# Second and third stage of a Fourier filter: 64x32 and 32x64 tiles on TensorE, the complex sum on VectorE

## The chip, the cores and the metric

The kernel runs on one core of a Trainium2 chip. A core has TensorE (PE in the profiles; its weight loads are shown apart as PEld), VectorE (DVE), ScalarE (ACT), GpSimd (POOL) and SyncE (SP), which work side by side and wait for each other by semaphores, and a set of DMA queues. Matrix products go from SBUF into PSUM, which VectorE and ScalarE empty. The metric is the device time of one execution in microseconds: the median of several runs.

## What is computed

```python
def _attn_ref(x, filt_r, filt_i):          # x: 8 x 3008 x 256, filters: 1505 x 256
    X = np.fft.rfft(x, axis=1)
    F = (filt_r + 1j * filt_i)[None, :, :]
    Y = X * F
    y = np.fft.irfft(Y, n=x.shape[1], axis=1)
    return y.astype(np.float32)

def _moe_ref(x, w_in, w_out):              # x: 24064 x 256, w_in: 256 x 2048
    h = x @ w_in
    g = 0.5 * h * (1.0 + erf(h / sqrt(2)))
    return (g @ w_out).astype(np.float32)
```

Each of the 8 batches is filtered along its 3008 positions by a real Fourier transform, a product with one complex filter per frequency and channel, and the transform back. The result, 24064 rows in all, goes through a two-layer network with GELU.

## The kernel before

The transform of length 3008 = 47 x 64 is made of small matrix products. A batch passes four stages: `s1` (47-point sums, tiles of 47x64), `s2` (64-point sums that give the spectrum), the product with the filter, `s3` (64-point sums back) and `s4` (47-point sums back, which write the rows that the network reads). Between `s1` and `s2`, and between `s3` and `s4`, the data goes through DRAM (`R1`, `R2`) to change its layout. `fold` ahead of `s1` forms sums and differences of input rows on VectorE. Batch 0 has a path of its own (`c1` to `c4`), ahead of everything else; it shares buffers and the filter tile `F` with the others.

The network works in 47 tiles of 512 rows: `mm1` (L635) writes the hidden layer into PSUM banks of the kind `h` (three of them), ScalarE applies GELU (L638), and `mm2_seven` multiplies by `w_out` with seven products in place of eight, which needs sums of operands on VectorE (`sums_1` L676, `sums_2` L682, `sums_3` L689) and several combinations of its results (L722 to L736), which empty the two banks `ps_o`. There are three more banks, of the kind `f`, which the Fourier stages use, together with one `h` bank where they need four.

The order is written out by hand: the program is a list of slots, 16 for each tile of 512 rows (a slot takes some 0.83 us where nothing else is put in), and `put(slot, function, ...)` at the end of the kernel puts the Fourier work of batches 1 to 7 into slots between the network's. Every engine runs its instructions strictly in the order in which they were put.

What the change touches, per batch, in three rounds `u` = 0, 1, 2:

- `r1` (L441) reads `R1` into `b_sb`: four transfers of 384 KB, six frequencies each. Three are put in the same slot, the fourth one slot after the first round's `s2`, when a buffer has come free.
- `s2` (L448, matmuls at L458): 16 matmuls with 64 rows and 64 columns of weights (`T2p`) and 256 moving columns, in four tiles of the array. The 64 columns of weights are real and imaginary parts of one group of frequencies, so real and imaginary parts lie on different partitions of the four PSUM banks.
- `s2_out` (L462, VectorE at L470), four times a round, in slots 0, 2, 4 and 6 after `s2`: one bank, multiplied once by the real and once by the imaginary part of the filter (`F[:, 0]` and `F[:, 1]`, 1024 elements per partition in all), into the tile `p12`.
- `s3` (L473, matmuls at L484), 9 or 10 slots after `s2`: 16 matmuls with 64 rows and 64 columns of weights (`U`) and 512 moving columns. The 64 rows hold real and imaginary parts, and two matmuls that add into one bank (`t` = 0 and 1) take the two filter parts, so the sums of the complex product are made inside the matrix product.
- `s3_out` (L490) copies the four banks to SBUF on ScalarE (L329; one on VectorE) and writes them to `R2` from SP.
- `load_filters_again` (L129): after batch 0, `F` is filled anew in the layout that batches 1 to 7 need, from a copy in DRAM, by GpSimd's queue (slot 1) and SP's (slot 18).
- `load_next` (L151): a tiny copy on GpSimd (`gate`, L149) that waits for a product of `s2_out` holds back the loads of the next batch.

Of the kernel before, what the change touches and what calls it, by code (L numbers as in the profile page):

```python
# [10 lines left out]
ALU = mybir.AluOpType  # L11
FP32 = mybir.dt.float32
BF16 = mybir.dt.bfloat16
# [5 lines left out]
NA, NB = 47, 64  # L19
K1 = 24  # L20
# [11 lines left out]
class _Mix:  # L32
    def __init__(self, ctx, tc, x, filt_r, filt_i, w_in, w_out, out):
# [10 lines left out]
        self.pa = pool("pa", 3)  # L44
        self.pb = pool("pb", 3)
        self.pp = pool("pp", 3)
# [82 lines left out]
    def load_filters_again(self, eng, k0, k):  # L129

        for o in range(0, 128, 32):
            i = self.st["Fd"][o // 64, :, :, :, k0:k0 + k, :].rearrange("q i t k c -> (q i) t k c")
            f = self.F[o:o + 32, :, k0:k0 + k, :]
            if o < 64:
                eng.dma_start(out=f.rearrange("p t k c -> p t (k c)"), in_=i.rearrange("p t k c -> p t (k c)"))
            else:
                for t in range(2):
                    for e in range(2):
                        eng.dma_start(out=f[:, t, e::2], in_=i[:, t, 1 - e::2])

# [10 lines left out]
    def load_next(self, b, p, c, h):  # L151

        self.gate(self.st[b, "p", p][0:1, 0, 0:1])
        self.load_x_pairs(b + 1, c, h)
# [95 lines left out]
    def weights_4(self, g):  # L250


        ts = self.nc.gpsimd.tensor_scalar
        h, q, self.wt, self.wts = (g.tile([128, 1], FP32, name=n) for n in ("h48", "q48", "wt", "wts"))
        ts(out=h, in0=self.p, scalar1=48.0, scalar2=None, op0=ALU.is_ge)
        ts(out=q, in0=h, scalar1=-48.0, scalar2=-1.5, op0=ALU.mult, op1=ALU.add)
        self.nc.gpsimd.tensor_tensor(out=q, in0=self.p, in1=q, op=ALU.add)
        self.nc.gpsimd.tensor_tensor(out=q, in0=q, in1=q, op=ALU.mult)
        ts(out=q, in0=q, scalar1=2.25, scalar2=-1.0, op0=ALU.is_equal, op1=ALU.mult)
        ts(out=self.wt, in0=q, scalar1=2.0, scalar2=None, op0=ALU.add)  # L260
        ts(out=h, in0=h, scalar1=-2.0, scalar2=1.0, op0=ALU.mult, op1=ALU.add)
        self.nc.gpsimd.tensor_tensor(out=self.wts, in0=self.wt, in1=h, op=ALU.mult)
# [97 lines left out]
    def table_u_pick(self, g):  # L360
        to = self.cols
        self.nc.gpsimd.iota(to, pattern=[[0, 2], [64, 2], [33, 2], [2, 16]], base=0, channel_multiplier=0,
                            allow_small_or_imprecise_dtypes=True)
        self.pick = g.tile([128, 128], BF16, name="pick")
        self.nc.gpsimd.tensor_scalar(out=self.pick, in0=to, scalar1=self.p, scalar2=None, op0=ALU.is_equal)
# [7 lines left out]
    def table_4_rows(self, g):  # L373

        v = self.nc.gpsimd
        self.t4 = g.tile([96, 224], FP32, name="t4_sb")
        self.T1g = g.tile([NA, 2, 2, 12, 2, 2], BF16, name="T1g")
        self.T2g = g.tile([128, 2, 12, 2, 2], BF16, name="T2g")
        for x in range(2):
            for r in range(2):  # L380
                t = self.T1[0:NA, 24 * (x ^ r):24 * (x ^ r) + 24].rearrange("p (a k) -> p a k", k=2)
                for j in range(2):
                    v.tensor_copy(out=self.T1g[:, x, r, :, j], in_=t[:, :, ::-1] if j else t)
        t = self.T2.rearrange("p (a k) r j -> p r a j k", k=2)[:, 0, :, 0:2, :]
        for r in range(2):
            for j in range(2):
                v.tensor_copy(out=self.T2g[:, r, :, j], in_=t[:, :, j, ::-1] if j else t[:, :, j])

    def table_4_factors(self, g):
        ps = self.bank("ps_t4", "f")  # L390
        mm = lambda o, n, t, k: self.nc.tensor.matmul(ps[0:96, o:o + n], lhsT=t, rhs=self.eye[0:k, 0:k], start=True, stop=True)
        for x in range(2):
            mm(NA * x, NA, self.T1g[:, x].rearrange("p r a j k -> p (r a j k)"), NA)
        mm(128, 128, self.T2g.rearrange("p r a j k -> p (r a j k)"), 128)
        t = self.t4
# [44 lines left out]

    def r1(self, b, c):  # L441
        bt = self.pb.tile([128, 6, 256], BF16, tag="b", name="b_sb")
        self.st[b, "b", c] = bt
        v = self.st[b, "R1"].rearrange("n (r k) c -> (n r) k c", r=2)
        self.nc.sync.dma_start(out=bt, in_=v[:, 6 * c:6 * c + 6, :])


    def s2(self, b, u):  # L448

        nc = self.nc  # L450
        self.st[b, "ps2"] = ps = [[self.bank("ps_s2", "h" if i == d == 0 else "f") for d in range(2)] for i in range(2)]
        for i in range(2):
            for j in range(2):
                for odd in range(2):
                    for d in range(2):
                        k, r = 8 * u + 4 * i + 2 * j + odd, slice(64 * d, 64 * d + 64)
                        o = 64 * (odd ^ d)
                        nc.tensor.matmul(ps[i][d][o:o + 64, 256 * j:256 * j + 256],  # L458
                                         lhsT=self.T2p[r, k].rearrange("p a b c -> p (a b c)"),
                                         rhs=self.st[b, "b", k // 6][r, k % 6, :], start=True, stop=True)  # L460

    def s2_out(self, b, u, i, d):  # L462

        if d == 0:
            w = self.st[b, "w"] = self.pp.tile([128, 2, 4, 256], BF16, tag="p12", name="p12")
            for q in range(2):
                self.st[b, "p", 4 * u + 2 * i + q] = w[:, :, 2 * q:2 * q + 2].rearrange("p t a c -> p t (a c)")
        k = 8 * u + 4 * i + d
        ps = self.st[b, "ps2"][i][d].rearrange("p (a c) -> p a c", a=2)
        self.nc.vector.tensor_tensor(out=self.st[b, "w"][:, :, d:4:2, :], in0=ps.unsqueeze(1).to_broadcast([128, 2, 2, 256]),  # L470
                                     in1=self.F[:, :, k:k + 3:2, :], op=ALU.mult)

    def s3(self, b, u):  # L473

        nc = self.nc
        if u == 0:
            self.st[b, "R2"] = self.dram.tile([NB, 12, 4, 256], BF16, tag="R2", name="R2")
        ps = [[self.bank("ps_s3", "h" if i == par == 0 else "f") for par in range(2)] for i in range(2)]
        for i in range(2):
            for t in range(2):  # L480
                for q in range(2):
                    for par in range(2):
                        r = slice(64 * par, 64 * par + 64)
                        nc.tensor.matmul(ps[i][par][64 * q:64 * q + 64, :],  # L484
                                         lhsT=self.U[r, t].rearrange("p r w -> p (r w)"),
                                         rhs=self.st[b, "p", 4 * u + 2 * i + q][r, t, :], start=t == 0, stop=t == 1)
        self.st[b, "ps3"] = ps
        self.s3_out(b, u, 0)

    def s3_out(self, b, u, i):  # L490
        ps = self.st[b, "ps3"][i]
        vt = self.pv.tile([128, 4, 256], BF16, tag="v", name="v_sb")
        for par in range(2):
            self._evac(vt[:, 2 * par:2 * par + 2, :].rearrange("p a b -> p (a b)"), ps[par],
                       False if b == u == i == par == 1 else "act")
        for q in range(2):
            self.nc.sync.dma_start(out=self.st[b, "R2"][:, 4 * u + 2 * i + q], in_=vt[64 * q:64 * q + 64])

# [40 lines left out]
    def c1t(self, q, eng):  # L539

        b = self.st[0, "b", q] = self.pb.tile([128, 6, 256], BF16, tag="b", name="b_sb")
        ps = self.bank("ps_c1t", "n", BF16)
        for i in range(8):
            self.nc.tensor.transpose(ps[:, 128 * i:128 * i + 128],
                                     self.at[:, i % 2, 4 * q + i // 2].rearrange("c h n r -> c (h n r)"), self.eye)
        n = 1024 // len(eng)
        for i, e in enumerate(eng):
            self._evac(b[:, 0:4, :].rearrange("p a b -> p (a b)")[:, n * i:n * i + n], ps[:, n * i:n * i + n], e)

# [226 lines left out]
def kernel(  # L776
# [14 lines left out]
    g = m.small  # L791
# [112 lines left out]
    def put(slot, f, *a):  # L904
        at.setdefault(slot, []).append((f, a))
# [5 lines left out]
    for b in range(1, B):  # L911
# [5 lines left out]
        for c in range(4):  # L917
            slot = s1 + int(c * n1 + (b == 1 and c in (1, 2)))
            put((0, 1, 5, 8)[c] if b == 1 else (67, 69, 86, 94)[c] if b == 2 else s1 - 28 + e + 6 * c, m.fold, b, c)
            put(slot, m.s1, b, c)  # L920
            put(r1 if c < 3 else s2[0] + 1, m.r1, b, c)
        for u in range(3):
            put(s2[u], m.s2, b, u)
            for i in range(4):
                put(s2[u] + ((0, 2, 5, 6)[i] if b == u == 1 else 2 * i + (b == 2 and u == 0)), m.s2_out, b, u, i // 2, i % 2)
            s3 = s2[u] + (9 if b == 1 and u != 1 else 10)
# [40 lines left out]
    for i, slot in enumerate((15, 80, 96, 112)):  # L967
        put(slot, m.table_4_all, parts[2 * i:2 * i + 2])
    put(1, m.load_filters_again, nc.gpsimd, 0, 8)
    put(18, m.load_filters_again, nc.sync, 8, 16)  # L970
    put(20, m.weight_sums)
# [53 lines left out]
```

## Time and profile before

| | |
|---|---|
| runs | 744.07, 744.24, 745.28 us; median 744.24 |
| profiled execution | 743.4 us; its span from first to last instruction 741.6 us; mean granted clock 1.000 |
| second stage, L458 | 336 matmuls of 64x64x256, busy 13.4 us |
| third stage, L484 | 336 matmuls of 64x64x512, busy 22.2 us |
| products, L470 | 84 of 1024 elements, 1217 ns each, busy 102.0 us |
| bf16 sums of folding, L106 and L107 | 1024 elements, 680 to 717 ns each |
| network's first layer, L635 | busy 445.4 us; GELU, L638: 446.6 us, 602 ns each |
| F<-Fd, transfers | POOL: 2 of 256 KB and 8 of 64 KB; SP: 2 of 512 KB and 8 of 128 KB |
| b_sb<-R | 28 of 384 KB, 3.9 us to landing |

The page gives each engine's busy time and, as a chain, the work that ended last, followed back in time. The timeline lists instructions in order of their start, neighbours of one line merged. A number in brackets at the end of its lines is the idle time of the engine just before, with what ended it; a line without brackets followed the one ahead of it without a pause. An instruction's shown length reaches a little over the start of the next where the two don't depend on each other.

### The profile page before, as it was taken

The page shows a single profiled execution, that of the slowest core. Times are in us where ns is not written, and L with a number is a line of the kernel's source. Part 1 is how long each engine was busy: PE and PEld are TensorE (multiplying, and loading weights), DVE is VectorE, ACT ScalarE, POOL GpSimd, SP SyncE. Part 2 cuts the span into 40 slices and gives each one's busy share as a digit, 9 for nine tenths or more (in the row PEclk, how much of TensorE's full clock was granted, in tenths as well). Part 3 has the DMA queues.
Part 4 walks back from the last instruction along what each step waited for, and adds up shares of the span by engine and source line. Part 5 has one row for each costly group of instructions (what it writes and reads, how often), then busy time and mean ns, then how long its engine had stood idle before and what let it go on. Part 6 is the DMA issues. An engine that isn't in the chain of part 4 may idle for free.

```text
span 741.6 us, 20996 instructions
## 1 busy us (share of the span) xinstructions
PE 731.2 (99%) x8588; PEld 507.9 (68%) x8588; DVE 584.7 (79%) x1036; ACT 574.6 (77%) x1048; POOL 292.9 (39%) x546
## 2 busy tenths in 40 slices
PE   7999999999999999999999999999999999999997
PEld 4856665666776666666777666666677666777776
DVE  7986988889877897788976889678888887675666
ACT  6997778678877888777887778877888778777773
POOL 7995356674313452135511364115531212121121
PEclk9999999999999999999999999999999999999999
DMA  9999643646265643645626555255545443311011
GB/s 150 224 201 233 163 110 97 194 102 140 76 156 143 133 101 98 188 100 125 133 85 171 120 116 137 74 156 141 110 100 136 137 111 106 92 45 43 31 58 58
DMA packets 84051, 90.79 MB, mean 122 GB/s; under 512 B 13347, under 2 KB 63011, under 8 KB 83827
## 3 DMA queue, kind: packets, MB, share of 16 engines
q1 hardware_dynamic: 61011, 49.11, 25.8%
q0 software_dynamic: 22528, 40.15, 24.3%
q8 instruction: 67, 1.10, 0.6%
q14 instruction: 29, 0.24, 0.1%
q10 hardware_dynamic: 416, 0.20, 0.1%
HBM read 57.15 MB, written 48.23 MB: 142 GB/s over the span
## 4 chain that ended last, share of the span: by engine, by line
PE 93%; DVE 3%; ACT 2%; DMA 1%; POOL 0%; issue 0%; DVEq 0%; POOLq 0%
PE ps_h L635 42%; PE ps_o L707 39%; PE ps_s L484 3%; PE ps_s L513 3%; PE ps_s L429 2%; PE ps_s L458 2%; PE ps_o L648 1%; DMA x_sb<-in_x_dram 1%; PE ps_c L582 1%; ACT y_sb L329 1%; ACT g_sb L638 1%; DVE g_sb L682 1%; DVE s_sb L676 1%; PE ps_c L560 0%; PE ps_warm L323 0%
## 5 line engine op out<-in xcount | busy, mean ns | idle before, releaser
L638 ACT ACTIVATE g_sb<-ps_h 128x512 f16<-128x512 f32 x752 | 446.6, 602 | 146.3 <-PE ps_h L635 143.5
L635 PE MATMUL ps_h<-y_sb,w_in_sb 128*128 128x512 bf16 (+3 forms) x1600 | 445.4, 366 | 0.2 <-DVE a_sb L331 0.2
L754 POOL DMA_DIRECT2D out_dram<-ost x227 | 128.8, 574 | 389.4 <-DVE ost L736 368.6
L707 PEld LDWEIGHTS <-g_sb 128*128 128x128 f16 x2944 | 193.9, 98 | 83.6 <-issue 11.6
L707 PEld LDWEIGHTS <-s_sb 128*128 128x128 f16 x2208 | 148.0, 98 | 62.0 <-issue 11.1
L635 PEld LDWEIGHTS <-w_in_sb 128*128 128x128 bf16 x1600 | 125.1, 98 | 7.2 <-issue 1.1
L707 PE MATMUL ps_o<-w_sums,g_sb 128*128 128x128 f16 x1472 | 127.4, 219 | 1.1 <-DVE g_sb L682 0.9
L707 PE MATMUL ps_o<-w_sums,s_sb 128*128 128x128 f16 x1472 | 126.2, 219 | 0.0
L676 DVE TENSOR_TENSOR s_sb<-g_sb 128x1024 f16<-128x1024 f16 x184 | 120.5, 689 | 1.0 <-ACT g_sb L638 1.0
L707 PE MATMUL ps_o<-w_out_sb,g_sb 128*128 128x128 f16 x1472 | 118.9, 219 | 0.0
L470 DVE TENSOR_TENSOR p<-ps_s,F 128x1024 bf16<-128x1024 f32 x84 | 102.0, 1217 | 5.4 <-PE ps_s L458 4.0
L98 POOL DMA_DIRECT2D x_sb<-in_x_dram x156 | 79.0, 513 | 1.1 <-PE ps_c3t L597 0.8
L729 DVE TENSOR_TENSOR t_sb<-t_sb,ps_o 128x256 f32<-128x256 f32 x46 | 19.3, 420 | 60.2 <-PE ps_o L707 60.2
L682 DVE TENSOR_TENSOR g_sb<-s_sb,g_sb 128x1024 f16<-128x1024 f16 x92 | 65.0, 707 | 1.6
L689 DVE TENSOR_TENSOR s_sb<-g_sb 128x1024 f16<-128x1024 f16 x92 | 64.1, 696 | 0.0
L707 PE MATMUL ps_o<-w_out_sb,s_sb 128*128 128x128 f16 x736 | 63.8, 219 | 0.0
L736 DVE TENSOR_TENSOR ost<-t_sb,ps_o 128x256 f32<-128x256 f32 x90 | 33.7, 416 | 20.5 <-PE ps_o L707 20.5
L513 PEld LDWEIGHTS <-d_sb 96*128 96x128 bf16 x448 | 31.9, 98 | 25.3
L329 ACT ACTIVATE y_sb<-ps_s 128x376 bf16<-128x376 f32 x94 | 46.7, 497 | 3.2 <-PE ps_s L513 3.2
L329 ACT ACTIVATE v_sb<-ps_s 128x512 bf16<-128x512 f32 x83 | 45.0, 597 | 0.2
L331 DVE CAST a_sb<-ps_s 128x512 bf16<-128x512 f32 x54 | 34.7, 684 | 12.7 <-PE ps_s L429 12.4
L724 DVE TENSOR_TENSOR ost<-t_sb,ps_o 128x256 f32<-128x256 f32 x46 | 19.1, 415 | 26.1 <-PE ps_o L707 26.1
(155 smaller groups left out, 526.8 us busy)
## 6 DMA issues: line engine op xcount, KB each, us to landing
out_dram<-ost POOLq DMA_DIRECT2D x125, 128.0 KB, 2.3
b_sb<-R SPq DMA_DIRECT2D x28, 384.0 KB, 3.9
R<-v_sb SPq DMA_DIRECT2D x84, 128.0 KB, 2.4
d_sb<-R SPq DMA_DIRECT2D x56, 192.0 KB, 3.4
R<-a_sb SPq DMA_DIRECT2D x108, 96.0 KB, 2.2
x_sb<-in_x_dram POOLq DMA_DIRECT2D x48, 94.0 KB, 2.6
x_sb<-in_x_dram POOLq DMA_DIRECT2D x48, 48.0 KB, 2.7
x_sb<-in_x_dram POOLq DMA_DIRECT2D x12, 188.0 KB, 5.4
```

The costliest lines, as they stand in the source:

```text
L98: self.nc.gpsimd.dma_start(out=xt[64 * v + to:64 * v + to + m, h, 4 * c:4 * c + 4 * n, :], in_=xv[h][at:at + m, w:w + 4 * n, :])
L329: self.nc.scalar.activation(out=out, in_=in_, func=AF.Copy, scale=1.0 if scale is None else scale)
L331: self.nc.vector.tensor_copy(out=out, in_=in_)
L470: self.nc.vector.tensor_tensor(out=self.st[b, "w"][:, :, d:4:2, :], in0=ps.unsqueeze(1).to_broadcast([128, 2, 2, 256]), in1=self.F[:, :, k ...
L513: nc.tensor.matmul(ps[:, 94 * i:94 * i + 94], lhsT=d[:, (grp % 2) * 4 + i, 128 * half:128 * half + 128], rhs=self.T4a[:, 4 * grp + i], sta ...
L635: nc.tensor.matmul(ps[:, o:o + n], lhsT=w[:, dc], rhs=self.ring[:, dc, off:off + n], start=(dc == 0), stop=(dc == 1))
L638: nc.scalar.activation(out=self.st["g", t][:, jc, :], in_=ps, func=AF.Gelu)
L676: self.nc.vector.tensor_tensor(out=self.st["s", t][:, i:i + 2], in0=a, in1=b, op=ALU.subtract)
L682: self.nc.vector.tensor_tensor(out=a21[:, k], in0=self.st["s", t][:, k, 0], in1=a22[:, k], op=ALU.add)
L689: self.nc.vector.tensor_tensor(out=self.st["s4", t][:, k], in0=a12[:, k], in1=s2[:, k], op=ALU.subtract)
L707: nc.tensor.matmul(ps[:, (m + 1) % 2, sub, :], lhsT=a[:, i, 128 * sub:128 * sub + 128], rhs=b[:, i], start=i == 0, stop=i == 7)
L754: eng.dma_start(out=out, in_=tile_[lo - r0:lo - r0 + n])
```

## The change

For batches 1 to 7 the spectrum is laid out differently. In `s2` a matmul now takes 32 columns of weights, either those of the real (`x` = 0) or of the imaginary part (`x` = 1) of one parity of positions, and four groups of partitions hold four groups of frequencies, so that real and imaginary parts of a frequency lie side by side in one partition. There are 32 matmuls a round for 16, in tiles of 64x32. The filter product stays four instructions of 1024 elements a round; after every second one, two instructions are added that form the real part (a difference) and the imaginary part (a sum) of the complex product over 512 elements each, in place. `s3` then takes 32 rows (no more real and imaginary parts of the spectrum mixed in the rows) in tiles of 32x64: 16 matmuls of 512 columns as before, with the two passes `t` outermost. The lines of `R1` are read in six transfers of 256 KB (`pb` has four buffers of 4 x 256 in place of three of 6 x 256), and the filter tile holds each value once: a group of 32 partitions has 12 frequencies in place of 24. Tables (`table_u_pick`, `table_4_rows`, `table_4_factors`, `weights_4`) are put in the order that this needs, with as many instructions.

```diff
-        self.pb = pool("pb", 3)
+        self.pb = pool("pb", 4)
...
     def load_filters_again(self, eng, k0, k):
         for o in range(0, 128, 32):
-            i = self.st["Fd"][o // 64, :, :, :, k0:k0 + k, :].rearrange("q i t k c -> (q i) t k c")
-            f = self.F[o:o + 32, :, k0:k0 + k, :]
-            if o < 64:
-                eng.dma_start(out=f.rearrange("p t k c -> p t (k c)"), in_=i.rearrange("p t k c -> p t (k c)"))
-            else:
-                for t in range(2):
-                    for e in range(2):
-                        eng.dma_start(out=f[:, t, e::2], in_=i[:, t, 1 - e::2])
+            k1 = K1 // 2 * (o // 32 % 2) + k0
+            i = self.st["Fd"][o // 64, :, :, :, k1:k1 + k, :].rearrange("q i t k c -> (q i) t (k c)")
+            eng.dma_start(out=self.F[o:o + 32, :, k0:k0 + k, :].rearrange("p t k c -> p t (k c)"), in_=i)
...
     def load_next(self, b, p, c, h):
-        self.gate(self.st[b, "p", p][0:1, 0, 0:1])
+        self.gate(self.st[b, "p", p][0:1, 0:1])
...
-    def r1(self, b, c):
-        bt = self.pb.tile([128, 6, 256], BF16, tag="b", name="b_sb")
-        self.st[b, "b", c] = bt
-        v = self.st[b, "R1"].rearrange("n (r k) c -> (n r) k c", r=2)
-        self.nc.sync.dma_start(out=bt, in_=v[:, 6 * c:6 * c + 6, :])
+    def r1(self, b, u, e):
+        bt = self.pb.tile([128, 4, 256], BF16, tag="b", name="b_sb")
+        self.st[b, "b", u, e] = bt
+        v, k = self.st[b, "R1"].rearrange("n (r k) c -> (n r) k c", r=2), K1 // 2 * e + 4 * u
+        self.nc.sync.dma_start(out=bt, in_=v[:, k:k + 4, :])
...
     def s2(self, b, u):
-        for i in range(2):
-            for j in range(2):
+        for i in range(0, 4, 2):
+            for x in range(2):
                 for odd in range(2):
-                    for d in range(2):
-                        k, r = 8 * u + 4 * i + 2 * j + odd, slice(64 * d, 64 * d + 64)
-                        o = 64 * (odd ^ d)
-                        nc.tensor.matmul(ps[i][d][o:o + 64, 256 * j:256 * j + 256],
-                                         lhsT=self.T2p[r, k].rearrange("p a b c -> p (a b c)"),
-                                         rhs=self.st[b, "b", k // 6][r, k % 6, :], start=True, stop=True)
+                    for o in range(0, 128, 32):
+                        d, e = odd ^ (o // 64), o // 32 % 2
+                        r = slice(64 * d, 64 * d + 64)
+                        nc.tensor.matmul(ps[i + odd][o:o + 32, x],
+                                         lhsT=self.T2p[r, K1 // 2 * e + 4 * u + i + odd, x].rearrange("p q j -> p (q j)"),
+                                         rhs=self.st[b, "b", u, e][r, i + odd, :], start=True, stop=True)
...
-    def s2_out(self, b, u, i, d):
-        if d == 0:
-            w = self.st[b, "w"] = self.pp.tile([128, 2, 4, 256], BF16, tag="p12", name="p12")
...
-        self.nc.vector.tensor_tensor(out=self.st[b, "w"][:, :, d:4:2, :], in0=ps.unsqueeze(1).to_broadcast([128, 2, 2, 256]),
-                                     in1=self.F[:, :, k:k + 3:2, :], op=ALU.mult)
+    def s2_out(self, b, u, i):
+        if i % 2 == 0:
+            self.st[b, "w"] = self.pp.tile([128, 2, 2, 2, 256], BF16, tag="p12", name="p12")
+        w, v = self.st[b, "w"], self.nc.vector.tensor_tensor
+        k = 4 * u + i
+        self.st[b, "p", k] = w[:, 1, 1, i % 2]
+        v(out=w[:, :, :, i % 2], in0=self.st[b, "ps2"][i].unsqueeze(1).to_broadcast([128, 2, 2, 256]),
+          in1=self.F[:, :, k].unsqueeze(2).to_broadcast([128, 2, 2, 256]), op=ALU.mult)
+        if i % 2:
+            self.st[b, "y", k // 2] = w
+            for t, op in ((0, ALU.subtract), (1, ALU.add)):
+                o, z = (w[:, t, x].rearrange("p a c -> p (a c)") for t, x in ((t, 0), (1 - t, 1)))
+                v(out=o, in0=o, in1=z, op=op)
...
     def s3(self, b, u):
-        for i in range(2):
-            for t in range(2):
-                for q in range(2):
-                    for par in range(2):
-                        r = slice(64 * par, 64 * par + 64)
-                        nc.tensor.matmul(ps[i][par][64 * q:64 * q + 64, :],
-                                         lhsT=self.U[r, t].rearrange("p r w -> p (r w)"),
-                                         rhs=self.st[b, "p", 4 * u + 2 * i + q][r, t, :], start=t == 0, stop=t == 1)
+        for t in range(2):
+            for q in range(2):
+                for o in range(0, 128, 32):
+                    r = slice(o, o + 32)
+                    nc.tensor.matmul(ps[o // 32][64 * q:64 * q + 64, :], lhsT=self.U[r, t].rearrange("p r w -> p (r w)"),
+                                     rhs=self.st[b, "y", 2 * u + q][r, t, 0].rearrange("p a c -> p (a c)"),
+                                     start=t == 0, stop=t == 1)
...
-            put(r1 if c < 3 else s2[0] + 1, m.r1, b, c)
+        for u in range(3):
+            for e in range(2):
+                put(r1 if u < 2 else s2[0] + 1, m.r1, b, u, e)
...
-    put(1, m.load_filters_again, nc.gpsimd, 0, 8)
-    put(18, m.load_filters_again, nc.sync, 8, 16)
+    put(1, m.load_filters_again, nc.gpsimd, 0, 4)
+    put(18, m.load_filters_again, nc.sync, 4, 8)
```

The slots of `s2`, `s2_out`, `s3` and `s3_out` stay as they are.

## The prediction

> **What bounds the kernel now.** I read the page's first two parts, then the chain that ended last, then the timeline of VectorE (DVE) and TensorE (PE) around the stages that the diff touches.
>
> ```profile
> PE 731.2 (99%) x8588; PEld 507.9 (68%) x8588; DVE 584.7 (79%) x1036; ACT 574.6 (77%) x1048; POOL 292.9 (39%) x546
> ...
> PE 93%; DVE 3%; ACT 2%; DMA 1%; POOL 0%; issue 0%; DVEq 0%; POOLq 0%
> ```
>
> PE runs without a break and its stream is the time: what shortens it is gained whole, what makes it wait is lost whole. DVE's 79% is an average. In order of time the chain shows what one of the 21 rounds (7 batches, 3 rounds each) costs PE:
>
> ```profile
> 410.10 0.56 PE ps_s L458 x16
> 410.66 0.50 PE ps_o L707 x7
> ...
> 418.99 0.99 PE ps_s L484 x16
> 419.98 0.50 PE ps_o L707 x7
> ```
>
> Columns: start, length, what. The second stage (L458) takes 0.56 us, the third (L484) 0.99. Between them DVE has to turn the one's banks into the other's operand; its timeline in that round (start, length, idle time in brackets):
>
> ```profile
> 413.62 1.22 DVE L470 TENSOR_TENSOR p<-ps_s,F 128x1024 bf16<-128x1024 f32 x1
> 414.76 0.41 DVE L722 COPY t_sb<-ps_o 128x256 f32<-128x256 f32 x1
> 415.09 1.21 DVE L470 TENSOR_TENSOR p<-ps_s,F 128x1024 bf16<-128x1024 f32 x1
> 416.22 0.68 DVE L689 TENSOR_TENSOR s_sb<-g_sb 128x1024 f16<-128x1024 f16 x1
> 416.82 1.22 DVE L470 TENSOR_TENSOR p<-ps_s,F 128x1024 bf16<-128x1024 f32 x1
> 417.95 0.41 DVE L724 TENSOR_TENSOR ost<-t_sb,ps_o 128x256 f32<-128x256 f32 x1
> 418.40 0.42 DVE L727 TENSOR_TENSOR t_sb<-t_sb,ps_o 128x256 f32<-128x256 f32 x1
> ```
>
> No bracket: from the first product to the last, DVE has no idle time. The last product ends at 418.04, PE begins the third stage at 418.92. This **slack of 0.88 us** is all that may be added to DVE here. I took it from the same rows in every round: 0.88 or 0.89 in ten; 1.25 in four (batches 3 and 4, round 3; 5 and 6, round 2); batch 1: -0.05, -0.31, 0.80 (negative, since its last product is needed only halfway through the stage); batch 2 round 1: 0.39; batch 7: 1.16, 2.12, 2.19.
>
> **The change part by part.** *Third stage.* Still 16 matmuls of 512 columns, but eight tiles of 32x64 abreast for four of 64x64. Now four rows of four start 0.216 us apart (418.92, 419.17, 419.38, 419.60): 0.86 us, and 0.13 until the next form starts. Two rows of eight: 0.43 + 0.13. Neighbouring matmuls of four abreast start 3 ns apart, so four more cost 0.015: 0.575 us. Gain 0.415 x 21 = **-8.7 us**.
>
> *Second stage.* 32 matmuls of 256 columns for 16, again eight abreast: still four rows of 0.109 us, so 0.56 + 0.015: **+0.3 us**. Nothing in this trace runs more than four tiles abreast. The bounds: 0.575, if eight run as four do; 0.99, if only four run (eight rows of 0.109, and 0.13). I take 0.575, since weights and matmuls of four tiles already interleave at 3 ns without holding each other up.
>
> The Trainium skill speaks against that: TensorE Tiling, "Restrictions and Gotchas", says that different row tiles cannot access one PSUM bank at the same time. Before, each bank was written by one row group; now each of the second stage's banks is written from both, into different partitions. No row of this trace shows such a pair. By the rule the stage would run four abreast and the sum would be that of the third rival below; by the 3 ns rows it stays at 0.575.
>
> *Products.* Four per round, 1024 elements from PSUM, as before: 1.217 us each, unchanged.
>
> *Sums.* New: four per round, 512 bf16 elements. Nearest rows: the bf16 sums of folding (L106, L107: 1024 elements, 680 to 717 ns) and the f32 product of 512 (L569: 678 ns). By the first, 417 ns (half of 533 ns streaming, and 150 fixed); by the second, 678. I take 417: operands and output are like L106's. An operation that waits for nothing starts 0.08 us before the one ahead ends, so a sum occupies 0.336. The first of a pair reads the product just issued: like L727 behind L724 (ended 418.37, next 418.40) it starts 0.034 after that end, not 0.08 before. A pair delays what is behind it by 0.115 + 2 x 0.336 = **0.787 us**, and two pairs stand ahead of the third stage: its operand is ready 1.57 us later. Without the wait a pair would cost 0.67; by L569's price, 1.31.
>
> *What waits.* PE's third stage waits in order; behind it stand L707 and L635, so the whole of PE stops (and ACT, which lives on L635). The final sum is needed 0.22 us into the stage (its second row), and PE follows DVE by 0.05 (L682 ended 111.04, L707 went on at 111.09). So the wait is 1.57 + 0.05 - 0.22 - slack = 1.40 - slack: ten times 0.52, four times 0.16, then 1.46, 1.71, 0.60, 1.01, 0.24 and twice none: **+10.9 us**.
>
> *What is late next.* L722, L724 and L727 empty two ps_o banks. L722 is one pair late; it comes before the third stage, and a wait there only takes the place of part of that wait. L727 has over 2 us to spare in most rounds. Not in round 3 of batches 2 to 6, where folding of the next batch lies ahead of it:
>
> ```profile
> 448.87 0.68 DVE L106 TENSOR_TENSOR xs<-x_sb 111x1024 bf16<-111x1024 bf16 x1
> 449.59 0.69 DVE L107 TENSOR_TENSOR x_sb<-x_sb 111x1024 bf16<-111x1024 bf16 x1
> 450.20 0.41 DVE L724 TENSOR_TENSOR ost<-t_sb,ps_o 128x256 f32<-128x256 f32 x1
> 450.64 0.42 DVE L727 TENSOR_TENSOR t_sb<-t_sb,ps_o 128x256 f32<-128x256 f32 x1
> ```
> ```profile
> 451.66 0.33 PE L707 MATMUL ps_o<-w_sums,s_sb 128*128 128x128 f16 x3
> 451.83 0.39 PE L707 MATMUL ps_o<-w_sums,g_sb 128*128 128x128 f16 x4
> ```
>
> The matmul at 451.83 is the first into the bank that L727 leaves at 451.06: 0.77 us (1.13 in batches 3 and 4). DVE comes 1.57 later, PE only by what the round has cost so far (0.52 - 0.415 = 0.1; with 1.13 us: 0.16 - 0.415 = -0.25). It waits 1.62 - 0.77 - 0.1 = 0.75 us, and as much in the other two: 5 x 0.75 = **+3.7 us**.
>
> *What costs nothing.* Reading the spectrum: six transfers of 256 KB for four of 384 KB, two more SP issues of about 0.35 us; SP mostly waits, and the last two are still issued as soon as the second stage's first round frees buffers, two rounds ahead of need. Filters: half the bytes, and six issues fewer on POOL and on SP; PE waits for neither in the list of waits. Tables: as many copies of as many elements. POOL's gates come about 1 us later, and the loads behind them are for the next batch, 12 us or more ahead of its folding. ACT's first copy of the third stage starts as before, 0.65 us after the stage's start; PE then asks for the next banks 0.415 earlier, and GELU frees them 0.9 us ahead. If these covers fail I allow 1 us.
>
> *The sum.* -8.7 + 0.3 + 10.9 + 3.7 = +6.2 us. The profiled execution took 743.4 us (span 741.6, 1.8 around it): 749.6. It is 0.8 below the median of 744.24, on whose scale this is about **750 us**.
>
> **The rivals.** *1. DVE keeps up, and the third stage's gain stays: faster.* This is decided at the third stage of the ten common rounds: the sums cost no wait if a pair delays by no more than (0.88 + 0.22 - 0.05) / 2 = 0.52 us instead of 0.787, that is, if a sum takes 0.26 us or doesn't wait for its product. At 0.52 there remain 2.7 us of waits in batches 1 and 2 and 3 us at L727's bank: -8.4 + 5.7 = -2.7, on the median's scale 741.5; with nothing left to wait for, 735.8. For it: DVE has idle time after each round (1.70 us ahead of L729). Against it: that is after the third stage, not ahead of it.
>
> *2. Break-even.* Pairs at 0.67: a quarter of a microsecond less in each round that waits gives +1.5 to +2, 746.
>
> *3. Eight tiles don't run abreast in the second stage.* It takes 0.99, 21 x 0.43 = +9.0 us. DVE's start slips by half of that, which takes 0.22 off each wait; the sum becomes +11, 755. If the third stage fails too, +17 to +18, 762.
>
> **How the numbers follow.** My forecast (waits exceed the gain) 0.58, its own range 747 to 753, from pairs of 0.70 to 0.85. Rival 1: 0.20. Rival 2: 0.09. Rival 3: 0.13, most of it at 755. The range of 741.5 to 756 leaves out half of rival 1 and the extremes of 3 (and sums at L569's price, near 770). A measurement here can't tell 0.2% (1.5 us) from no change. Faster: 0.20, rival 1. Same: 0.09, rival 2's share. Slower: 0.71.
>
> **What would show it.** In the profile after: the third stage's 16 matmuls 0.57 us from end to end (0.99: rival 3); the second stage 0.57; sums of some 417 ns; the first of a pair 0.03 us behind its product's end; PE idle ahead of the third stage, released by the sums' line, some 0.5 us in common rounds and over 1 us in batch 1; PE idle at L707, released by L727's successor, in round 3 of batches 2 to 6. A DVE busy time near 615 us. I am wrong if PE shows no idle time released by the sums, or if a pair delays by 0.5 us or less.

## The result, and the profile after

The changed kernel takes 752.47 us (median of 4 runs, 752.39 to 753.63) against 744.15 (4 runs, 743.88 to 745.28): ratio 1.0112, interval 1.0095 to 1.0130. It is 8.3 us slower. The profiled execution took 752.45 us (span 750.5) against 743.4 (741.6): 9.05 us more, and this is the difference that the working below has to account for.

The page of the changed kernel, its busy times and the shares of the chain that ended last:

```profile
PE 726.4 (97%) x8782; PEld 508.1 (68%) x8924; DVE 616.0 (82%) x1120; ACT 574.8 (77%) x1048; POOL 287.3 (38%) x540
...
PE 75%; DVE 15%; ACT 3%; issue 2%; DMA 2%; POOL 2%; DVEq 0%
```

The trace holds 8782 matmuls for 8924 weight loads (8588 for 8588 before): 142 records are missing, 138 of them of the first layer, and the idle time that they leave is not idle time of the engine. So PE's busy time can't be set beside the 731.2 of before. The chain can: VectorE had 3% of it and has 15%, and the kernel without sums, further down, with as many records missing, has 4%. PE now waits for VectorE.

The groups of the changed lines, with shapes kept apart (busy us and mean ns of one; then the idle time before them). L464 is the product, L470 the sums, L453 the second stage, L482 the third:

```profile
L464 DVE TENSOR_TENSOR p<-ps_s,F 128x1024 bf16<-128x1024 f32 x84 | 102.2, 1219 | 3.1 <-PE ps_s L453 1.6
L470 DVE TENSOR_TENSOR p<-p 128x512 bf16<-128x512 bf16 x84 | 33.0, 434 | 1.4
L482 PE MATMUL ps_s<-p,U 32*64 32x512 bf16 x336 | 20.9, 392 | 0.7 <-DVE p L464 0.5
```

A sum takes 434 ns, and the 84 of them are busy for 33.0 us, about the 31.3 us by which DVE's busy time grew. The third stage's busy time fell by only 1.3 us (22.2 to 20.9), because the shown lengths of the matmuls that have started the stage, some 390 ns each, reach over the wait of the later ones for their operand. What one round costs is seen in PE's timeline, in the round that the prediction used (start, length):

```profile
426.81 0.59 PE L633 MATMUL ps_h<-y_sb,w_in_sb 128*128 128x512 bf16 x2
427.34 1.02 PE L482 MATMUL ps_s<-p,U 32*64 32x512 bf16 x16
428.29 0.56 PE L705 MATMUL ps_o<-w_sums,s_sb 128*128 128x128 f16 x7
```

From the stage's start to the next matmul it is 428.29 - 427.34 = 0.95 us; it was 0.99. Where nothing waits (batch 7, rounds 2 and 3) the same distance is 0.57. So here 0.385 us of the stage is waiting, inside the group, and no bracket shows it. VectorE in the same round:

```profile
421.89 1.22 DVE L464 TENSOR_TENSOR p<-ps_s,F 128x1024 bf16<-128x1024 f32 x1
423.14 0.76 DVE L470 TENSOR_TENSOR p<-p 128x512 bf16<-128x512 bf16 x2
423.82 0.42 DVE L720 COPY t_sb<-ps_o 128x256 f32<-128x256 f32 x1
424.15 1.22 DVE L464 TENSOR_TENSOR p<-ps_s,F 128x1024 bf16<-128x1024 f32 x1
425.28 0.68 DVE L687 TENSOR_TENSOR s_sb<-g_sb 128x1024 f16<-128x1024 f16 x1
425.88 1.22 DVE L464 TENSOR_TENSOR p<-ps_s,F 128x1024 bf16<-128x1024 f32 x1
427.14 0.76 DVE L470 TENSOR_TENSOR p<-p 128x512 bf16<-128x512 bf16 x2
427.81 0.41 DVE L722 TENSOR_TENSOR ost<-t_sb,ps_o 128x256 f32<-128x256 f32 x1
428.26 0.42 DVE L725 TENSOR_TENSOR t_sb<-t_sb,ps_o 128x256 f32<-128x256 f32 x1
```

From a product to the evacuation behind its pair of sums it is 423.82 - 421.89 = 1.93 us, where it was 1.14: a pair delays by 0.79. The last pair ends at 427.90, half a microsecond after PE has begun the stage that reads it.

The waits that the prediction did not have are brackets in PE's timeline, in batch 1 round 3, batch 2 round 1 and batch 7 round 1:

```profile
100.80 0.45 PE L705 MATMUL ps_o<-w_out_sb,g_sb 128*128 128x128 f16 x5 [0.64 <-DVE ost L734]
...
154.32 0.34 PE L511 MATMUL ps_s<-T4a,d_sb 96*128 96x94 bf16 x4 [1.68 <-DVE p L464]
...
603.78 0.44 PE L705 MATMUL ps_o<-w_out_sb,g_sb 128*128 128x128 f16 x5 [0.64 <-DVE ost L734]
```

The first and the last are a bank that L734 empties, with a pair of sums ahead of it on DVE. The middle one is the fourth stage, which wants a bank of kind `f` that a late product still holds. There VectorE itself was slow:

```profile
148.74 1.22 DVE L464 TENSOR_TENSOR p<-ps_s,F 128x1024 bf16<-128x1024 f32 x1
149.99 1.83 DVE L470 TENSOR_TENSOR p<-p 128x512 bf16<-128x512 bf16 x2
151.74 1.30 DVE L687 TENSOR_TENSOR s_sb<-g_sb 128x1024 f16<-128x1024 f16 x1
152.97 1.21 DVE L464 TENSOR_TENSOR p<-ps_s,F 128x1024 bf16<-128x1024 f32 x1
```

A pair takes 1.83 us for 0.76, and L687 1.30 for 0.68, while GpSimd builds the fourth stage's table beside them:

```profile
148.78 1.62 POOL L405 TENSOR_TENSOR tmp_sb<-t_sb 96x376 f32<-96x376 f32 x2
150.48 1.05 POOL L407 TENSOR_TENSOR T4a<-tmp_sb 96x376 bf16<-96x376 f32 x1
151.62 2.12 POOL L405 TENSOR_TENSOR tmp_sb<-t_sb 96x376 f32<-96x376 f32 x2
```

### The profile page after: what moved, and what is told of

It reads as the page before. It is cut to its first block, busy times and chain, and to the rows that moved or that the text cites. A ratio compares the mean times of both kernels' runs of the same rounds, so it can differ in the third digit from the quotient of the medians.

```text
span 750.5 us, 21598 instructions
## 1 busy us (share of the span) xinstructions
PE 726.4 (97%) x8782; PEld 508.1 (68%) x8924; DVE 616.0 (82%) x1120; ACT 574.8 (77%) x1048; POOL 287.3 (38%) x540
## 3 DMA queue, kind: packets, MB, share of 16 engines
q8 instruction: 70, 1.15, 0.6%
## 4 chain that ended last, share of the span: by engine, by line
PE 75%; DVE 15%; ACT 3%; issue 2%; DMA 2%; POOL 2%; DVEq 0%
PE ps_o L705 33%; PE ps_h L633 31%; DVE p L464 5%; PE ps_s L511 3%; PE ps_s L424 2%; ACT g_sb L636 2%; PE ps_s L482 2%; DVE s_sb L674 2%; DVE p L470 1%; POOL out_dram L752 1%; DMA x_sb<-in_x_dram 1%; ACT v_sb L324 1%; PE ps_s L453 1%; PE ps_o L646 1%; DVE g_sb L680 1%
## 5 line engine op out<-in xcount | busy, mean ns | idle before, releaser
L633 PE MATMUL ps_h<-y_sb,w_in_sb 128*128 128x512 bf16 (+3 forms) x1462 | 415.8, 365 | 0.6 <-DVE a_sb L326 0.2
L674 DVE TENSOR_TENSOR s_sb<-g_sb 128x1024 f16<-128x1024 f16 x184 | 119.7, 685 | 0.9 <-ACT g_sb L636 0.9
L464 DVE TENSOR_TENSOR p<-ps_s,F 128x1024 bf16<-128x1024 f32 x84 | 102.2, 1219 | 3.1 <-PE ps_s L453 1.6
L687 DVE TENSOR_TENSOR s_sb<-g_sb 128x1024 f16<-128x1024 f16 x92 | 63.9, 694 | 0.0
L727 DVE TENSOR_TENSOR t_sb<-t_sb,ps_o 128x256 f32<-128x256 f32 x46 | 19.3, 420 | 41.9 <-PE ps_o L705 41.9
L734 DVE TENSOR_TENSOR ost<-t_sb,ps_o 128x256 f32<-128x256 f32 x90 | 33.7, 417 | 18.4 <-PE ps_o L705 18.4
L511 PE MATMUL ps_s<-T4a,d_sb 96*128 96x94 bf16 x448 | 38.1, 206 | 2.6 <-DVE p L464 1.7
```

The costliest lines, as they stand in the source:

```text
L464: v(out=w[:, :, :, i % 2], in0=self.st[b, "ps2"][i].unsqueeze(1).to_broadcast([128, 2, 2, 256]), in1=self.F[:, :, k].unsqueeze(2).to_broad ...
L511: nc.tensor.matmul(ps[:, 94 * i:94 * i + 94], lhsT=d[:, (grp % 2) * 4 + i, 128 * half:128 * half + 128], rhs=self.T4a[:, 4 * grp + i], sta ...
L633: nc.tensor.matmul(ps[:, o:o + n], lhsT=w[:, dc], rhs=self.ring[:, dc, off:off + n], start=(dc == 0), stop=(dc == 1))
L674: self.nc.vector.tensor_tensor(out=self.st["s", t][:, i:i + 2], in0=a, in1=b, op=ALU.subtract)
L687: self.nc.vector.tensor_tensor(out=self.st["s4", t][:, k], in0=a12[:, k], in1=s2[:, k], op=ALU.subtract)
```

## The experiments

Eight kernels ran, the first four on one chip (the kernel before there: 743.84 us) and the last four on another (744.03); ratios are to these, and plain differences between kernels of different series carry the 0.3 us by which the kernel before differs among them. The loss of a round, below, is by how much PE falls behind the kernel before from this round's second stage to the next round's; it is read from the starts of the network's second-layer matmuls, which are the same in both profiled executions. The theory: VectorE's sums, 0.79 us a pair, make TensorE wait, and take back more than the new third stage gives.

**No sums.** In `s2_out` of the changed kernel the loop goes.

```diff
-            for t, op in ((0, ALU.subtract), (1, ALU.add)):
-                o, z = (w[:, t, x].rearrange("p a c -> p (a c)") for t, x in ((t, 0), (1 - t, 1)))
-                v(out=o, in0=o, in1=z, op=op)
```

> The changed kernel without the difference and the sum on VectorE (84 instructions less): the output lacks the cross terms of the complex product. Theory (all of the loss is PE waiting for what VectorE does late because of the sums; the tile forms themselves are a gain): nothing of the waits is left, third stage 0.57 us in all 21 rounds, 744.2 - 8.7 + 0.3 = 735.8 us (735 to 737.5). Rival (the new tile forms, the new reads of R1 or the new filter loads cost something themselves): 740 us or more.

735.94 us, ratio 0.9897 (0.9882 to 0.9912). Each group of third-stage matmuls, shapes kept apart:

```profile
L479 PE MATMUL ps_s<-p,U 32*64 32x512 bf16 x336 | 13.8, 386 | 0.0
```

The stage is busy 13.8 us for 22.2 before and 20.9 with the sums. It takes 0.570 in every round but batch 1's first two, and from batch 2 round 1 on each round brings PE 0.42 us forward of the kernel before. So the new tiles alone, with the new reads and filter loads, are worth 7.9 us, and the sums cost 8.3 + 7.9 = 16.2.

**The sums twice.** Each line is issued a second time.

```diff
                 v(out=o, in0=o, in1=z, op=op)
+                v(out=o, in0=o, in1=z, op=op)
```

> Each sum is issued twice (the second adds or subtracts once more, so the output has the cross terms twice). Theory (VectorE's time ahead of the third stage sets the wait): a pair delays by another 0.67 us, a round by 1.34 us, and every one of the 19 rounds that wait now loses all of it: 752.5 + 19 x 1.34 = 778 us, a little more where VectorE no longer catches up between rounds (776 to 786). Rival (the wait comes from the semaphores and the order, not from VectorE's time): 752 to 760 us.

796.5 us (794.0 to 798.0), ratio 1.0718 (1.0700 to 1.0736): slower as foretold, by more than foretold. VectorE's timeline, a doubled pair in a round of batch 5:

```profile
448.55 0.42 DVE L470 TENSOR_TENSOR p<-p 128x512 bf16<-128x512 bf16 x1
449.01 0.42 DVE L471 TENSOR_TENSOR p<-p 128x512 bf16<-128x512 bf16 x1
449.35 0.42 DVE L470 TENSOR_TENSOR p<-p 128x512 bf16<-128x512 bf16 x1
449.80 0.42 DVE L471 TENSOR_TENSOR p<-p 128x512 bf16<-128x512 bf16 x1
450.14 0.41 DVE L721 COPY t_sb<-ps_o 128x256 f32<-128x256 f32 x1
```

A repeated sum reads what the one before it wrote, so it starts 0.46 us after it and not 0.34. From the first sum to the evacuation it is 1.59 us, where it was 0.68: a doubled pair delays by 0.91 us more, and the expectation counted 0.67. Two pairs in 21 rounds are 2 x 0.91 x 21 = 38 us, which gives 791, and common rounds lose just that, 1.94 us for 0.11. Two rounds lose more: batch 2 round 1, 6.5 us for 1.89 (2.8 beyond the doubled pairs), and batch 1 round 3, 4.0 for 1.0 (1.2 beyond). Most of this is not VectorE's: TensorE's granted clock, 1.00 throughout in the changed kernel, is 0.50 here from 104.8 to 108.2 us and from 166.2 to 169.6, just behind the third stages of these two rounds, which take 2.96 and 5.08 us. In the first stretch PE falls back by 1.2 us, in the second by 1.5; another 0.9 in batch 2 round 1 is a wait of the second stage for `b_sb`, and some 0.4 is left for sums that GpSimd stretches. Why the clock fell there and not behind other long stages (3.86 us in batch 1 round 1) is open. In common rounds each further microsecond on VectorE ahead of the third stage is lost once TensorE waits.

**The same sums in the kernel before.** After every second product of the old kernel, a difference and a sum of the same size, in place.

```diff
+        if d:
+            w = self.st[b, "w"]
+            for t, op in ((0, ALU.subtract), (1, ALU.add)):
+                o, z = w[:, t, 0:2].rearrange("p a c -> p (a c)"), w[:, 1 - t, 2:4].rearrange("p a c -> p (a c)")
+                self.nc.vector.tensor_tensor(out=o, in0=o, in1=z, op=op)
```

> The kernel before, with a difference and a sum of 512 bf16 elements in place after every second product, at the same places in VectorE's order as in the changed kernel (the output then has terms mixed that don't belong together). Theory, by the same steps as the prediction: the old third stage needs the late operand only 0.45 us (difference) and 0.66 us (sum) after its start, so in common rounds it doesn't wait; what is left are the banks that VectorE empties late: 0.14 us in ten common rounds, 0.5 to 0.85 in round 3 of batches 2 to 6, 1 to 2 in batch 1 and in batch 2 round 1, 0.6 in batch 7 round 1: together some +10 us, 754.5 us (752 to 757). Rival (the shorter third stage is a full gain of 8.4 us that simply adds to the cost of the sums): 752.5 + 8.4 = 761 us.

754.69 us (754.17 to 755.29), ratio 1.0149 (1.0134 to 1.0164), as the theory has it; the rival that adds the parts up (761) falls. PE's timeline in batch 5 round 1:

```profile
427.79 1.09 PE L489 MATMUL ps_s<-p,U 64*64 64x512 bf16 x16
428.81 0.56 PE L712 MATMUL ps_o<-w_sums,s_sb 128*128 128x128 f16 x7
```

With the sums ahead of it the old third stage takes 1.02 us and the new one 0.95. The old stage is slow to reach its late operand anyway: it waits 0.03 where the new one waits 0.385. The faster stage is worth 7.9 us alone, and only 754.7 - 752.5 = 2.2 beside the sums; for the rest it has the wait in its place.

**The third stage later.** Its slot goes two back in batches 2 to 6, behind the wait.

```diff
-            s3 = s2[u] + (9 if b == 1 and u != 1 else 10)
+            s3 = s2[u] + (9 if b == 1 and u != 1 else 12 if 1 < b < B - 1 else 10)
```

> The changed kernel with the third stage two slots later (12 in place of 10 after the second stage) in batches 2 to 6. Theory: the wait of some 0.38 us ahead of the third stage goes in the rounds 1 and 2 that have it, the waits at the banks of ps_o stay, above all in round 3 of each batch, where L725 lies behind the folding: 752.5 - 3.1 = 749.4 us (748.3 to 750.5). Rival (the wait only moves to what comes next, for VectorE lacks time over the whole round): 752 us or more.

754.54 us (753.72 to 754.68), ratio 1.0145 (1.0129 to 1.0160): the theory's number is wrong, and the rival, that the wait only moves, is right. PE's timeline in batch 5 round 1:

```profile
428.63 0.33 PE L705 MATMUL ps_o<-w_sums,s_sb 128*128 128x128 f16 x3
429.12 0.40 PE L705 MATMUL ps_o<-w_sums,g_sb 128*128 128x128 f16 x4 [0.16 <-DVE t_sb L725]
429.35 0.59 PE L633 MATMUL ps_h<-y_sb,w_in_sb 128*128 128x512 bf16 x2
429.88 0.64 PE L482 MATMUL ps_s<-p,U 32*64 32x512 bf16 x16
430.45 0.56 PE L705 MATMUL ps_o<-w_sums,g_sb 128*128 128x128 f16 x7
```

The third stage is at its 0.57 in all 15 rounds that were moved. But a matmul ahead of it waits for the bank that L725 empties: from the three matmuls to the four behind them it is 0.49 us, 0.17 in the changed kernel (the bracket shows only part of the wait). Common rounds lose 0.06 us in place of 0.11, and round 3 of each of the five batches 0.5 more than in the changed kernel: 5 x 0.5 - 10 x 0.05 = 2.0, as far as the medians lie apart (2.1). The two profiled executions differ by 1.3: this one also loses 0.4 us less ahead of the first changed round, and 0.5 less in batch 2 round 1, where a wait for `b_sb` has come in the place of others. The list of waits of this kernel, and then of the changed one (waiting line, what it waited for: us in total, times, longest):

```profile
PE ps_o L705 <- DVE t_sb L725: 8.2, 12, 1.5
```
```profile
PE ps_o L705 <- DVE t_sb L725: 3.1, 5, 0.6
```

In the kernel before, L727 (here L725) left its bank 2 us ahead of need, and I took that for room. The third stage's own 0.99 us lay between the two and was part of it: take the stage out from there and the room goes with it. What is late is VectorE, by two pairs, and whoever asks for its results first pays.

**Half of each sum.** 256 of the 512 elements.

```diff
-                v(out=o, in0=o, in1=z, op=op)
+                v(out=o[:, 0:256], in0=o[:, 0:256], in1=z[:, 0:256], op=op)
```

> Each sum over 256 of its 512 elements (half of the cross terms are left out). A pair then delays by about 0.115 + 2 x 0.20 = 0.52 us, the point that the prediction named as the one from which the common rounds no longer wait at the third stage. Theory: third stage 0.57 to 0.60 us in the ten common rounds; waits stay in batch 1, in batch 2 round 1 and, of 0.3 us, in round 3 of batches 2, 5 and 6; sum -0.8 us against the kernel before: 743.4 us (742 to 745). Rival (each added instruction costs PE by itself, whatever its length): 750 us or more.

740.7 us (740.18 to 741.13), ratio 0.9953 (0.9938 to 0.9967): below the expectation of 742 to 745. VectorE and PE in batch 5 round 1:

```profile
417.71 0.48 DVE L470 TENSOR_TENSOR p<-p 128x256 bf16<-128x256 bf16 x2
418.11 0.41 DVE L722 TENSOR_TENSOR ost<-t_sb,ps_o 128x256 f32<-128x256 f32 x1
```
```profile
418.27 0.64 PE L482 MATMUL ps_s<-p,U 32*64 32x512 bf16 x16
```

A pair delays by 0.51 us (0.11 and 0.40 from its start to L722's) in place of 0.79, and the third stage runs at 0.57 in all rounds of batches 3 to 7. So with a pair of 0.51 us the common rounds don't wait, and with one of 0.79 they wait 0.52: this fits the 0.52 us a pair that the prediction's first rival named, though nothing between 0.51 and 0.79 was run. The rival's own number for that case, 741.5, was 0.8 too high. The expectation of this run was further off and its sum isn't itemized, so where it failed is open. By rounds the ten common ones gain 0.42 us each, batch 1 loses 0.27, 0.53 and 0.22, and batch 2 round 1 loses 0.62, with 1.0 us of waiting for `b_sb` in it.

**GpSimd's table later.** The last of four pieces of table work goes from slot 112 to 123.

```diff
-    for i, slot in enumerate((15, 80, 96, 112)):
+    for i, slot in enumerate((15, 80, 96, 123)):
```

> The changed kernel with the last part of GpSimd's table_4_all at slot 123 in place of 112, out of batch 2 round 1, where a pair of sums took 1.83 us and not 0.76. Theory: there the sums and L687 go back to 0.76 and 0.68 us, PE's wait of 1.68 us at L511 (a bank that the late third product holds) goes, and 0.4 us at the third stage stay: 752.5 - 1.5 = 751.0 us, less what GpSimd stretches at its new place (750.7 to 752). Rival (the pair was long for another reason): its length and the time stay, 752.5 us.

751.65 us (750.99 to 751.77), ratio 1.0097 (1.0080 to 1.0114). VectorE in batch 2 round 1, and then where GpSimd's work now runs:

```profile
149.84 0.76 DVE L470 TENSOR_TENSOR p<-p 128x512 bf16<-128x512 bf16 x2
150.51 0.69 DVE L687 TENSOR_TENSOR s_sb<-g_sb 128x1024 f16<-128x1024 f16 x1
...
156.94 3.99 DVE L674 TENSOR_TENSOR s_sb<-g_sb 128x1024 f16<-128x1024 f16 x3
```

The sums are back at 0.76, the 1.68 us wait is gone, and the round's loss falls from 1.89 to 0.19 us. But three additions at L674 take 3.99 where three take 1.89 elsewhere, and the next round loses 1.26. What stretches VectorE is GpSimd's work, wherever it lies. Of the 1.7 us that one round gained, the next lost 1.15 more than in the changed kernel, and the median is 0.8 lower, with intervals of the two kernels that overlap.

**The sums behind the evacuations.** The sums become a function of their own, all four in a row, put behind the evacuations of the `ps_o` banks; the third stage goes back by one or two slots (in batch 1 by up to two), and the first folding of batches 3 to 6, which lay ahead of L725 in round 3 of the batch before, goes three slots back (that of batch 7 stays).

```diff
+    def s2_sum(self, b, u):
+        for q in range(2):
+            w = self.st[b, "y", 2 * u + q]
+            for t, op in ((0, ALU.subtract), (1, ALU.add)):
+                o, z = (w[:, t, x].rearrange("p a c -> p (a c)") for t, x in ((t, 0), (1 - t, 1)))
+                self.nc.vector.tensor_tensor(out=o, in0=o, in1=z, op=op)
...
-            put((0, 1, 5, 8)[c] if b == 1 else (67, 69, 86, 94)[c] if b == 2 else s1 - 28 + e + 6 * c, m.fold, b, c)
+            put((0, 1, 5, 8)[c] if b == 1 else (67, 69, 86, 94)[c] if b == 2 else s1 - 28 + e + 6 * c + 3 * (c == 0 and e == 0), m.fold, b, c)
...
-            s3 = s2[u] + (9 if b == 1 and u != 1 else 10)
+            put(s2[u] + (7 if b == 1 else 8), m.s2_sum, b, u)
+            s3 = s2[u] + ((10, 10, 11)[u] if b == 1 else 11 if b == B - 1 else 12)
```

> The changed kernel with all four sums of a round in a function of their own, eight slots after the second stage (seven in batch 1), behind L722 and L725, so that no bank is emptied late because of them; third stage at 10, 10, 11 slots in batch 1, 12 in batches 2 to 6, 11 in batch 7; the first folding of the next batch three slots later, behind the sums. Theory (only what stands ahead of something that PE awaits costs time): waits are left only in batch 1 (about 0.9 us net) and the gain of 0.415 us stays in nearly all others: 744 - 6.6 = 737.5 us (736 to 741). Rival (VectorE lacks the time over the whole round, wherever the sums stand): 747 us or more.

740.84 us (739.63 to 741.74), ratio 0.9954 (0.9939 to 0.9969), at the upper end of what was expected and faster than both kernels. VectorE in batch 5 round 1:

```profile
417.12 0.41 DVE L727 TENSOR_TENSOR ost<-t_sb,ps_o 128x256 f32<-128x256 f32 x1
417.57 0.42 DVE L730 TENSOR_TENSOR t_sb<-t_sb,ps_o 128x256 f32<-128x256 f32 x1
417.90 1.42 DVE L475 TENSOR_TENSOR p<-p 128x512 bf16<-128x512 bf16 x4
419.25 0.68 DVE L692 TENSOR_TENSOR s_sb<-g_sb 128x1024 f16<-128x1024 f16 x1
```

Both evacuations (L727, L730 here) now come ahead of the sums, and the four sums take 1.35 us from first start to L692's: none of them waits for a product just issued, so a pair is 0.67. The third stage is at 0.57 in all rounds of batches 2 to 6 but two (0.625, and 0.92 in batch 6 round 3, where the folding was left). 4.9 us above the kernel without sums remain. Batch 1 loses 1.4 us where it gains 0.75 without sums, batches 2 to 6 gain 4.3 of 6.3, and batch 7's first two rounds lose 0.5 in place of gaining 0.8; other slots there were not tried.

**The same with folding left where it was.**

```diff
-            put((0, 1, 5, 8)[c] if b == 1 else (67, 69, 86, 94)[c] if b == 2 else s1 - 28 + e + 6 * c + 3 * (c == 0 and e == 0), m.fold, b, c)
+            put((0, 1, 5, 8)[c] if b == 1 else (67, 69, 86, 94)[c] if b == 2 else s1 - 28 + e + 6 * c, m.fold, b, c)
```

> The same with the folding left where it was, ahead of L722 and L725 in round 3 of batches 2 to 6. Theory: with the third stage behind it, PE comes to the bank that L725 empties about 1 us earlier than before and waits up to 0.2 to 0.5 us in these five rounds: 1 to 2.5 us more than the version with the folding moved. Rival (folding doesn't matter): equal.

742.26 us (740.74 to 742.80), ratio 0.9974 (0.9962 to 0.9985): 1.4 us above the run before, inside the 1 to 2.5 that were expected, though the two intervals overlap. But the time is not lost where the theory has it. From batch 2 round 2 on each round loses the same in the two profiled executions, to 0.01 us (round 3 of batches 2 to 6: 0.16, -0.20, -0.20, 0.16 and -0.02 in both). The folding does hold up the third stage, by 0.20 to 0.35 us in the four rounds from which it had been moved, but PE makes up for it before the round is over: the rival, that folding doesn't matter, is right there. The two executions differ by 1.7 us (742.29 and 740.58), and all of it arises earlier: 1.1 in batch 1 round 3, behind a wait of the fourth stage for `d_sb` (0.85), and 1.2 in batch 2 round 1, less 0.6 ahead of the first changed round. PE in batch 2 round 1, in the run before and then in this one:

```profile
143.13 0.63 PE L453 MATMUL ps_s<-b_sb,T2p 64*32 64x256 bf16 x32
```
```profile
143.64 0.28 PE L453 MATMUL ps_s<-b_sb,T2p 64*32 64x256 bf16 x1
144.86 0.63 PE L453 MATMUL ps_s<-b_sb,T2p 64*32 64x256 bf16 x31 [0.94 <-DMA b_sb<-R]
```

The second stage waits there for a transfer from `R1`. That these waits come from the folding, all of which was put later, isn't shown.

## Why the prediction came out as it did

The sign, the mechanism and the range were right; the number was 2.5 us short of the median, and the sum 2.85 short of the profiled execution's 9.05. One sign that the prediction asked for did not show in its own words: no row of the changed kernel has PE idle ahead of the third stage with the sums as releaser. The stage starts and then waits inside its group of matmuls, so that its length alone, 0.95 us, would have looked like the third rival's 0.99. It is the kernel without sums, at 0.57, that tells the wait from slow tiles.

*Third stage, -8.7 us.* Right: 0.570 without a wait, for 0.575. The kernel without sums shows what this is worth when it is not waited away, 7.9 us.

*Second stage, +0.3 us.* 32 matmuls take 0.563 us in every round but one (batch 1 round 3: 0.815, and 0.76 before), as 16 did: nothing. The rule of the Trainium skill (TensorEngine Tiling, "Restrictions and Gotchas") that different row tiles cannot access one PSUM bank at the same time is not borne out here as a matter of time: a bank written from both row groups, into different partitions, cost not even the 0.015 us that was allowed. The third rival falls with it.

*The pair of sums, 0.787 us.* Measured 0.79, from 434 ns a sum where 417 was estimated; with half-size sums a pair of 0.51 no longer makes common rounds wait.

*Waits at the third stage, +10.9 us.* Right by rounds, though not all of it stood there. In a common round the stage waits 0.385 us, and another 0.14 falls earlier, where PE takes the bank that L720 empties. Together 0.52, as worked out; with the gain taken off, a common round loses 0.11 us (0.105 foretold). Batch 1's first two rounds lose 1.04 and 1.30 (1.05 and 1.30 foretold).

*L727's bank, +3.7 us.* The list of waits of the changed kernel has just these: five, 3.1 us in all. Round 3 of a batch loses 0.52 us in batches 3 and 4 and 0.90 in 2, 5 and 6, with 0.49 and 0.85 foretold.

*What is late next.* This is the step that failed, and with it 2.9 us were left out. It looked at L722, L724 and L727 and at no other bank that VectorE frees behind the sums. In batch 1 round 3 and batch 7 round 1 it is L736's bank (L734 after) that comes late, and each of these rounds loses 0.8 us more than foretold. In batch 2 round 1 it is an `f` bank which the fourth stage wants, with the sums stretched by GpSimd: 1.29 more. 0.8 + 0.8 + 1.29 = 2.9, the missing amount within 0.1. (Shifts of +0.56 before the first changed round and -0.64 after the last cancel; other runs of nearly the same program have other values there.) The stretching could have been read beforehand, in VectorE's timeline of the kernel before, in that very round:

```profile
145.96 1.10 DVE L689 TENSOR_TENSOR s_sb<-g_sb 128x1024 f16<-128x1024 f16 x1
...
150.03 1.16 DVE L689 TENSOR_TENSOR s_sb<-g_sb 128x1024 f16<-128x1024 f16 x1
```

These take 0.68 elsewhere. I took only the slack from this round and not the speed at which the new work would run in it.

*Reading the spectrum, nothing.* This held in the profiled execution of the changed kernel. In four of the eight experiments (doubled sums, third stage later, half sums, folding left) the second stage of batch 2 round 1 waits for `b_sb` after its first matmul and takes 1.49 to 1.77 us in place of 0.56. Neither of the two traces with the old reads has this wait; whether the new transfers cause it was not tested.

*"L727 has over 2 us to spare in most rounds"* was true where it stood, but it counted the third stage as spare time. That did no harm to the prediction; it did to the expectation of the run with the third stage later, 5 us off.

## What to carry to other kernels

Work given to a second engine costs the path of the first as soon as it exceeds the slack between the two at that place, round by round, and not by the second engine's busy share: here 79% busy on average had 0.88 us of room where 1.57 were put. List every buffer that the now later engine frees behind the new work, and who asks first, and count no instruction that you mean to speed up or move as room. Moving the consumer alone only moved the wait to the next buffer here; putting the new work behind the evacuations that others wait for, and the consumer behind it, took 11.6 us off, with the same instructions.

## What the runs showed of the hardware

- Two 512-element bf16 sums on VectorE took 1.83 us beside GpSimd's additions and multiplications and 0.76 without, and an f16 sum of 1024 elements 1.30 for 0.68. The products in the same stretch, with one operand in PSUM, kept to 1.21 and 1.22. This agrees with the Trainium skill (SBUF — State Buffer, "Who interferes with whom"): a VectorE instruction with two SBUF inputs contends with a GpSimd instruction that reads SBUF, and one with at most one SBUF input, outside the modes that use both ports, does not.
- Eight tiles of 64x32, two row groups writing different partitions of one PSUM bank, ran abreast: 32 matmuls of 256 columns in 0.563 us.
- A VectorE instruction that reads the output of the one just ahead starts 0.03 to 0.04 us after that one's end, one that doesn't starts 0.08 before it: 0.46 and 0.34 us from start to start for a sum of 512.
